# Attention and a SwiGLU block in one kernel: output-weight sums of 768 columns at other places, one load moved between two others, three small moves and a third store queue at the end

## The chip, the core and the metric

The kernel runs on one core of one Trainium2 chip. The metric is the device time of one execution in microseconds (us). A core has five engines, each with its own program and its own order: TensorE (PE; its weight loads, PEld, run beside its matmuls), VectorE (DVE), ScalarE (ACT), GpSimd (POOL) and SyncE (SP). SP, ACT and POOL can ask for DMA transfers. TensorE's results lie in PSUM, whose banks are handed round among the tiles of a pool: a tile can be written when the last reader of its bank's former tile is done.

## The reference

```
scores = q @ k.T / sqrt(64)              # 8 batches, 12 heads, 448 tokens, 64 columns a head
attn   = softmax(scores)
x      = (attn @ v), heads side by side  # 3584 tokens x 768
g      = x @ w_gate                      # 768 x 1536
out    = (g * sigmoid(g) * (x @ w_val)) @ w_out   # 1536 x 768
```

Inputs and output are float32. The kernel computes in float16 with float32 accumulation; transfers issued by POOL convert on the way.

## The kernel before

**Attention.** Two heads make a pair; there are 48 pairs, six to a batch. `load_qk16` and `load_v` let POOL fetch q, k and v. For pairs 0 to 10, `prep` turns q and k with TensorE (L249, L272); from pair 11 on POOL copies them into one tile (L231, L208) and SP issues DMA transposes (L234 to L240; L210 and L214). `qk` multiplies keys by queries a chunk of keys at a time (L329; from pair 12 on L299, and L311 for the chunk that two pairs share) and ACT takes the exponential of each (L337, L319). `pv` multiplies by the values with a column of ones (L355, L363, L390), takes the reciprocal of the sums (L374, L415) and scales (L376, L416). The result is turned into X, 768 x tokens: with TensorE and a copy (`turn_x`, L446 and L453) for pairs below 12, by SP's transposes (L455, L459) behind. In the first two batches the last 64 columns of each pair are turned together by `turn_rests` (L472, L479).

**The SwiGLU block.** Tokens go in eight blocks of 384 or 512. A `Step` is one block with 128 of the 1536 hidden columns: six matmuls for the gate, six for the value (L513), a tanh on ACT (L537), the product `t` = (tanh + 1) x gate (L553), and the product `hts` of `t` and the value (L561), both on DVE. `run_fv` runs one step; `run_pair` runs two whose gates stand ahead of both values.

**The output.** Block 0 and single chunks are multiplied plainly (`plain_out`, L581 and L588). All else goes by groups (`out_group`): 2 x 2 blocks of tokens and hidden halves are multiplied with seven products in the place of eight (L610), from sums of hidden values (`h_sums`, L498 to L501) and sums of output weights (`out_sums`, L487 to L490), which are made once. The parts are put together by ACT (L650, L629) and DVE (L651, L653, L657, L663). The next six matmuls of TensorE behind L657 overwrite what L657 reads.

**Where the sums are made.** The order on every engine is written out by hand. Sums stand in the lists `wsums` and `sums`; `add_sum` takes the next from `sums` and puts it at that place in DVE's order. `run_o`, which runs one output step of block 0, moves four of `wsums` and makes them when less than two output steps are left; the others are made inside the steps of block 1 in the same manner as the sums of hidden values later. One weight sum takes the 384 columns of one of six pairs of hidden blocks.

**The order of the loads.** POOL issues DMAs in program order, and its transfers land in that order here. `wq` names the pair at whose entry the weights are asked for: `("o", 0)` at pair 6, `("o", 1)` at pair 7, 1152 KB each. On the entry of pair 8 the kernel asks for q and k of pair 14 (`load_qk16(pr + LA, 1)`, LA = 6). In the program as built, POOL's DMAs take eight semaphores in turn, so that a DMA waits for the landing of the one eight places before it.

**The end.** The last group runs two halves of the columns side by side. Each of its four parts, named by z (which 128 tokens) and qw (which half), is stored when it is ready, as two DMAs: z = 0, qw = 1 by ACT, the three others by SP.

Of the kernel before, what the change touches and what calls it, by code (L numbers as in the profile page):

```python
# [39 lines left out]
def kernel(  # L40
# [10 lines left out]
    nc = tc.nc  # L51
    B, H, S, D = q.shape
# [11 lines left out]
    OH = DM // 2  # L64
# [48 lines left out]
    NH = NFB // 2  # L113
# [3 lines left out]
    Tsum = [x.rearrange("p (c m) -> p c m", c=NH) for x in spare]  # L117
# [4 lines left out]
    QW = OH // 2  # L122

    wo_all = consts.tile([128, 2, NFB, OH], FP16, name="wo")
# [3 lines left out]
    qkT = {}  # L128
# [90 lines left out]
    def prep(pr):  # L219
        if pr >= QUAD:  # L220
            return prep_quad(pr)
        rq, rk = raw[pr]
        if pr == 0 or pr >= NPE:
            qk16 = attp.tile([128, 2, NC, 2, D], FP16, tag="qk16", name="qk16", bufs=3)[0:P]
            for t, src in enumerate((rq, rk)):
                dst = qk16[:, 1 - t].rearrange("p c h d -> p h c d")
                if pr == 0:
                    nc.vector.tensor_copy(dst[:, 0], src[:, 0])
                    nc.scalar.activation(dst[:, 1], src[:, 1], AF.Copy)
                else:  # L230
# [12 lines left out]

        def turn0():
            for t in range(2):
                tp = ps_s.tile([128, 2, 512], FP32, tag="s", name="tp")
                for c in range(NC):
                    for hx in range(2):
                        nc.tensor.matmul(  # L249
                            tp[ts(hx, 64), c // 2, ds(c % 2 * P, P)],  # L250
                            lhsT=qk16[:, 1 - t, c, hx],
                            rhs=ident[0:P, 0:P],
                            start=True,
                            stop=True,
                        )
                dst = qkT[pr][:, ts(1 - t, S)].rearrange("p (a x) -> p a x", a=2)
                nc.vector.tensor_copy(dst[:, 0], tp[:, 0, 0 : 2 * P])
                nc.scalar.activation(dst[:, 1], tp[:, 1, 0 : 2 * P], AF.Copy)
                if t == 0:
                    tq = tp  # L260
            nc.vector.tensor_copy(qkT[pr][:, 2 * S :], tq[:, 0, 0:D])

        def turn():
            if pr < FIRST + 2:
                tp = ps_s.tile([128, 2, 1024], FP16, tag="s", name="tp")[:, 0]
            else:
                tp = ps_f.tile([128, 1024], FP16, tag="f", name="tp")
            for i in range(2 * NC + 1):
                t, c = (1 - i // NC, i % NC) if i < 2 * NC else (0, 0)
                for hx in range(2):  # L270
                    src = raw[pr][t][:, hx, c, :]
                    nc.tensor.transpose(tp[ts(hx, 64), ts(i, P)], src, ident[0:P, 0:P])  # L272
            nc.vector.tensor_copy(qkT[pr][:], tp[:, 0 : 2 * S + D])

        return turn if pr else turn0
# [205 lines left out]
    gate_small = [False]  # L481

    def out_sums(c):
        b11, b12, b21, b22 = (wo_all[:, :, f, ts(i, QW)] for f in (c, NH + c) for i in range(2))
        t1, t2, t3, t4 = (t[:, c].rearrange("p (h m) -> p h m", h=2) for t in Tsum)
        return [
            lambda: nc.vector.tensor_sub(t1, b12, b11),  # L487
            lambda: nc.vector.tensor_sub(t2, b22, t1),
            lambda: nc.vector.tensor_sub(t3, b22, b12),
            lambda: nc.vector.tensor_sub(t4, b21, t2),  # L490
        ]
# [70 lines left out]
                self.hts[:, self.fb, 0:n], self.t1[:, 0:n], 0.5 * HS, self.vp[:, 0:n], ALU.mult, ALU.mult  # L562
            )

    def store(osb, kk, l0, n, m0, w, queue=nc.sync):
        l = l0
        while l < l0 + n:
            b, j = divmod(l, S)
            turned = D if b + NB * kk < QUAD // NHP else 0
            c, p0 = divmod((j + turned) % S, P)  # L570
            m = min(P - p0, l0 + n - l, (MQ if turned and j < MQ else S) - j)
            dst = out[ts(NB * kk + b, S), :].rearrange("(p c) m -> c p m", c=NC)[c, p0 : p0 + m]
            src = osb[l - l0 : l - l0 + m]
            queue.dma_start(dst[:, ds(m0, w)], src[:, ds(m0, w)])
            l += m

    def plain_out(kk, c0, hts, ch, m0, w, osb):
        op = ps_f.tile([128, 512], FP32, tag="f", name="op")
# [24 lines left out]
    def out_group(kk, c0, hts, t, qw, osb, last=False, own=False):  # L603
        x, y, w = ts(2 * t, 128), ts(2 * t + 1, 128), ts(qw, QW)
        g = ps_s.tile([128, 2, 512], FP32, tag="s", name="og")
        a, c, b = g[:, 0, 0:QW], g[:, 0, QW:OH], g[:, 1, 0:QW]
# [24 lines left out]
        def stored(z):  # L631
            l0 = c0 + (2 * t + z) * 128
            if last:
                store(osb[z], kk, l0, 128, qw * OH, OH, nc.sync if z or not qw else nc.scalar)
            elif qw:
                store(osb[z], kk, l0, 128, 0, DM)

# [19 lines left out]
        part = nc.vector.scalar_tensor_tensor(d, b, 1.0 / HS, p15[:], ALU.mult, ALU.add)  # L657
# [20 lines left out]
    with tc.manual_schedule():  # L678
# [6 lines left out]
        for vo in Vts:  # L685
# [19 lines left out]
            3: [("qk", 9, 1), ("qk", 10), ("g", 2), ("v", 2)],  # L705
            4: [("g", 3), ("v", 3), ("qk", 12)],
            6: [("V", 3), ("o", 0)],
            7: [("o", 1)],
        }

        def emit(item):
# [12 lines left out]

        groups = []
        sums = []
        wsums = [f for c in range(NH) for f in out_sums(c)]
        steps = []

        def pair_groups(kk, c0, hts, t, last=False):  # L730
# [38 lines left out]
        def add_sum(n=1):  # L769
            for _ in range(n):  # L770
                if sums:
                    sums.pop(0)()

        def run_fv(quiet=False, more=0):
            step = fvq.pop(0)
            step.gate()
            add_sum(more)
            step.value(0)
            if not quiet:
                add_sum()  # L780
            step.finish()
            if not quiet:
                add_sum()
            return 2 * step.time

        def run_pair(small=0):
            one, two = fvq.pop(0), fvq.pop(0)
            one.gate()
            two.gate()
            one.value(0)  # L790
            one.gated()
            two.gated()
            one.finish()
            add_sum(small)
            two.value(0)
            add_sum()
            two.finish()
            return 4 * one.time

# [8 lines left out]
        def run_o():  # L808
            gen, t = oq.pop(0)
            next(gen)  # L810
            if len(oq) < 2 and not groups and wsums:
                sums.extend(wsums[:4])
                wsums[:4] = []
                add_sum(4)
            return t

        def run_group(nf, inside=None, gate_first=False):
            gen = groups.pop(0)[0](gate_first)
            for _ in range(nf - 1):
                run_fv()  # L820
            step = fvq.pop(0)
            if gate_first:
                step.gate()
                add_sum()
            next(gen)
            if not gate_first:
                step.gate()
                add_sum()
            if inside:
                inside()  # L830
                next(gen)
            step.value(0)
            add_sum()
            step.finish()
            add_sum()
            if not inside:
                next(gen)

        def run_budget(budget):
            while (fvq or oq) and budget > 0:  # L840
                if not fvq:
                    budget -= run_o()
                elif len(fvq) > 1 and fvq[0].at[1] and 2 * fvq[0].time < budget <= 4 * fvq[0].time:
                    budget -= run_pair(1)
                else:
                    budget -= run_fv(more=1)
            return budget

        def left():
# [12 lines left out]
        for u in range(FIRST * NC):  # L862
            pr, c = divmod(u, NC)
# [22 lines left out]
        queue = []  # L886
# [12 lines left out]
        while g < last or queue:  # L899
            n = 2 if g < WIDE * NC else 3  # L900
# [16 lines left out]
        def open_products(rests):  # L917
            for p0 in rests:
                pv_open(p0)
                pv_rest(p0)  # L920
            return []
# [6 lines left out]
        for x, (chunks, todo) in enumerate(plan):  # L928
# [14 lines left out]
            for n, (pr, c) in enumerate(ordered):  # L943
                if n == 2 and after_group:
                    rests = open_products(rests)
                qk(pr, c)
            open_products(rests)
            end = min([y for y in adds if y > x] + [len(plan) + 1])
            if x == 0:
                turn_x(4)  # L950
# [40 lines left out]
            else:  # L991
# [10 lines left out]
                    run_steps(nf)  # L1002
                for _ in range(no):
                    run_o()
            if x == 1:
                turn_rests(0)
            while turns:
                turn_x(turns.pop(0))
            if XPE - 1 in [p0 for _, p0 in todo]:
# [54 lines left out]
```

## Time and profile before

| What | us |
|---|---|
| median of 3 runs (lowest, highest) | 445.86 (442.65, 447.48) |
| the profiled execution, its own time | 446.76 |
| its span from first to last instruction | 445.0 |
| TensorE busy, share of the span | 430.9 (97%) |
| VectorE, ScalarE, GpSimd busy | 263.3, 222.9, 180.2 |
| granted TensorE clock, mean | 0.994 |
| sums of output weights, L487 to L490, 24 of 384 columns | 13.2 busy |

Durations and places below come from the one profiled execution, in microseconds from the start of its span. The time of an execution is 1.8 us longer than the span. TensorE's "busy" holds matmuls one after the other; a gap in it is shown in brackets with what ended it. The "granted clock" is the share of its full clock that TensorE had in a stretch.

### The profile page before, as it was taken

The numbers are of one execution on the slowest core, as the hardware profiler recorded it, in microseconds if no ns is written. First come the engines' busy times: TensorE is split into PE (matmuls) and PEld (weight loads), VectorE is DVE, ScalarE is ACT, GpSimd is POOL, SyncE is SP. The second block draws the span as 40 slices with busy tenths as digits, with TensorE's granted clock in tenths as the row PEclk, the third lists the DMA queues.
The fourth block names the chain that finished last, engine by engine and source line by source line (L and its number), as shares of the span: only waits on it lengthen the run. The fifth ranks groups of instructions, "written<-read, shape, count | busy, mean of one in ns | idle before, by whom it ended". The sixth has DMA issues, their size and how long they took to land.

```text
span 445.0 us, 11025 instructions
## 1 busy us (share of the span) xinstructions
PE 430.9 (97%) x4456; PEld 274.9 (62%) x4456; DVE 263.3 (59%) x611; ACT 222.9 (50%) x332; POOL 180.2 (40%) x299
## 2 busy tenths in 40 slices
PE   8999999898999999999999999999999999999995
PEld 3665565544446686674756776774756778565494
DVE  4666562586777755655556755564556665654562
ACT  6975667455456546454545554546464642222221
POOL 8755714997874645535533362823000000000000
PEclk9999999899999999999999999999999999999999
DMA  9999999999999789984899669954142012202014
GB/s 138 189 199 201 199 173 144 149 199 184 134 140 96 89 135 125 160 106 67 109 132 125 89 99 139 160 107 66 34 109 53 12 42 62 73 1 72 0 41 140
DMA packets 108500, 49.98 MB, mean 112 GB/s; under 512 B 60832, under 2 KB 105120, under 8 KB 108448
## 3 DMA queue, kind: packets, MB, share of 16 engines
q0 software_dynamic: 46832, 24.56, 49.6%
q1 hardware_dynamic: 61456, 24.52, 30.6%
q8 instruction: 35, 0.57, 0.5%
q10 hardware_dynamic: 160, 0.20, 0.2%
q14 instruction: 17, 0.14, 0.1%
HBM read 49.55 MB, written 11.01 MB: 136 GB/s over the span
## 4 chain that ended last, share of the span: by engine, by line
PE 74%; DMA 13%; DVE 4%; POOL 4%; issue 2%; ACT 1%; SPq 0%; DVEq 0%; POOLq 0%
PE gp L513 21%; PE vp L513 20%; PE og L610 16%; PE acc L390 8%; DMA qkraw<-in_k_dram 5%; PE s L299 5%; DMA wv<-in_moe_w_val_dram 4%; PE op L581 4%; DMA wg<-in_moe_w_gate_dram 2%; POOL qkraw L171 2%; PE s L311 1%; DMA qkT<-qk 1%; ACT E L319 1%; DVE hts L561 1%; POOL vraw L182 1%
## 5 line engine op out<-in xcount | busy, mean ns | idle before, releaser
L513 PE MATMUL gp<-X,wg 128*128 128x384 f16 (+1 forms) x576 | 123.3, 353 | 0.0
L513 PE MATMUL vp<-X,wv 128*128 128x384 f16 (+1 forms) x576 | 123.2, 352 | 0.0
L319 ACT ACTIVATE E<-s 128x896 f16<-128x896 f32 x126 | 106.7, 917 | 32.5 <-PE s L299 20.5
L537 ACT ACTIVATE sg<-gp 128x384 f32<-128x384 f32 (+1 forms) x96 | 52.4, 546 | 92.2 <-PE gp L513 86.3
L553 DVE SCALAR_TENSOR_TENSOR t<-sg,gp 128x384 f32<-128x384 f32 (+1 forms) x96 | 59.5, 620 | 64.7 <-ACT sg L537 64.3
L513 PEld LDWEIGHTS <-wv 128*128 128x128 f16 x576 | 56.3, 98 | 51.9
L513 PEld LDWEIGHTS <-wg 128*128 128x128 f16 x576 | 53.6, 98 | 45.7 <-issue 2.6
L208 POOL COPY qk<-qkraw 128x512 f16<-128x512 f16 x72 | 43.6, 655 | 92.6 <-DMA qkT<-qk 91.5
L561 DVE SCALAR_TENSOR_TENSOR hts<-t,vp 128x384 f16<-128x384 f32 (+1 forms) x96 | 59.5, 620 | 8.9 <-PE vp L513 0.8
L148 POOL DMA_DIRECT2D vraw<-in_v_dram x72 | 44.6, 651 | 16.1 <-DVE xt L376 7.3
L390 PEld LDWEIGHTS <-E 128*128 128x128 f16 (+1 forms) x1152 | 37.8, 97 | 14.6 <-issue 8.7
L390 PE MATMUL acc<-vo,E 128*128 128x65 f16 (+1 forms) x1152 | 43.3, 193 | 3.0 <-DVE hts L561 3.0
L610 PEld LDWEIGHTS <-hts 128*128 128x128 f16 x528 | 44.0, 98 | 2.1 <-issue 1.1
L337 ACT ACTIVATE E<-s 112x896 f16<-112x896 f32 x48 | 40.7, 917 | 7.9 <-PE s L329 7.7
L148 POOL DMA_DIRECT2D qkraw<-in_k_dram x70 | 43.1, 641 | 2.3 <-DMA wg<-in_moe_w_gate_dram 1.2
L415 DVE RECIPROCAL R<-acc 128x4 f32<-128x4 f32 x72 | 12.7, 177 | 37.7 <-PE acc L390 37.6
L629 ACT ACTIVATE osb<-og 128x384 f32<-128x384 f32 x22 | 10.8, 491 | 45.3 <-PE og L610 38.8
L171 POOL DMA_DIRECT2D qkraw<-in_q_dram x44 | 30.6, 696 | 4.7 <-DMA vraw<-in_v_dram 1.2
L416 DVE TENSOR_TENSOR xt<-acc,R 128x256 f16<-128x256 f32 x72 | 30.5, 424 | 2.5
L299 PE MATMUL s<-qkT 64*128 64x448 f16 x216 | 30.0, 353 | 1.7 <-DMA qkT<-qk 1.7
L610 PE MATMUL og<-wo,hts 128*128 128x192 f16 x264 | 29.0, 246 | 0.0
L610 PEld LDWEIGHTS <-hsum 128*128 128x128 f16 x300 | 25.7, 98 | 2.3
(78 smaller groups left out, 391.5 us busy)
## 6 DMA issues: line engine op xcount, KB each, us to landing
vraw<-in_v_dram POOLq DMA_DIRECT2D x72, 64.0 KB, 4.7
qkraw<-in_q_dram POOLq DMA_DIRECT2D x41, 112.0 KB, 4.2
qkraw<-in_k_dram POOLq DMA_DIRECT2D x68, 64.0 KB, 4.4
wg<-in_moe_w_gate_dram POOLq DMA_DIRECT2D x8, 288.0 KB, 10.1
wv<-in_moe_w_val_dram POOLq DMA_DIRECT2D x8, 288.0 KB, 10.2
wo<-in_moe_w_out_dram POOLq DMA_DIRECT2D x2, 1152.0 KB, 20.2
out_dram<-osb SPq DMA_DIRECT2D x7, 288.0 KB, 4.2
out_dram<-osb SPq DMA_DIRECT2D x6, 336.0 KB, 3.4
```

The costliest lines, as they stand in the source:

```text
L148: eng.dma_start(dst[ts(s, 64)], rows)
L171: nc.gpsimd.dma_start(dst, flat.rearrange("h (p c) d -> p h (c d)", c=NC))
L208: nc.gpsimd.tensor_copy(dst.rearrange("p c h d -> p h c d"), src)
L299: nc.tensor.matmul(s[:, hx, 0:S], lhsT=t[ts(hx, 64), ts(c + low(pr, hx), 128)], rhs=t[ts(hx, 64), ds(NC * 128, S)], start=True, stop=True,)
L319: nc.scalar.activation(e[:, 0 : 2 * S].rearrange("p (h q) -> p h q", h=2), s[:, :, 0:S], AF.Exp, scale=sm_scale)
L337: nc.scalar.activation(e[:, :, 0:S], s[0:P, :, 0:S], AF.Exp, scale=sm_scale)
L390: nc.tensor.matmul(acc[:, ts(j, D + 1)], lhsT=e[rows, ds(hx * S + j * 128, 128)], rhs=Vts[pr % NV][rows, hx, col, 0 : D + 1], start=first, ...
L513: nc.tensor.matmul(dst[:, 0:n], lhsT=wslice(kind, self.fb, cb), rhs=X[kk][:, cb, ds(c0, n)], start=(cb == 0), stop=(cb == NCB - 1),)
L537: nc.scalar.activation(self.sg[:, 0:n], gp[:, 0:n], AF.Tanh, scale=0.5)
L553: nc.vector.scalar_tensor_tensor(self.t1[:, 0:n], self.sg[:, 0:n], 1.0, self.gp[:, 0:n], ALU.add, ALU.mult)
L561: nc.vector.scalar_tensor_tensor(self.hts[:, self.fb, 0:n], self.t1[:, 0:n], 0.5 * HS, self.vp[:, 0:n], ALU.mult, ALU.mult)
L610: nc.tensor.matmul(dst, lhsT=lhs(n), rhs=rhs(n), start=first and n == 0, stop=n == NH - 1, skip_group_check=True)
```

## The change

Seven places are edited.

1. `out_sums` takes two hidden blocks at once, so that a sum has 768 columns and there are 12; their order is now the first two kinds for all columns, then the last two. `run_o` moves three at a time.
2. In `run_pair` with `small`, one sum stands between the two `t` products, and none between the two `hts`; `run_fv` has no extra sum behind the gate.
3. In `run_group` the last sum is made behind the end of the group (`next(gen)`).
4. The second output weight is asked for at pair 8, behind q and k of pair 14.
5. `turn_rests(0)` stands behind the scores of step 2, and no longer at the end of step 1.
6. In `turn0` the copy of the first 64 columns stands directly behind the first of the two copies.
7. In the last group's stores the larger of the two DMAs goes first, and the part z = 1, qw = 0 is issued by POOL.

```diff
-                if t == 0:
-                    tq = tp
-            nc.vector.tensor_copy(qkT[pr][:, 2 * S :], tq[:, 0, 0:D])
+                if t == 0:
+                    nc.vector.tensor_copy(qkT[pr][:, 2 * S :], tp[:, 0, 0:D])
...
     def out_sums(c):
-        b11, b12, b21, b22 = (wo_all[:, :, f, ts(i, QW)] for f in (c, NH + c) for i in range(2))
-        t1, t2, t3, t4 = (t[:, c].rearrange("p (h m) -> p h m", h=2) for t in Tsum)
+        b11, b12, b21, b22 = (
+            wo_all[:, :, ds(f, 2), ts(i, QW)].rearrange("p h c m -> p c h m") for f in (c, NH + c) for i in range(2)
+        )
+        t1, t2, t3, t4 = (t[:, ds(c, 2)].rearrange("p c (h m) -> p c h m", h=2) for t in Tsum)
...
+        if large_first:
+            parts.sort(key=lambda part: -part[0])
+        for _, dst, src in parts:
+            queue.dma_start(dst, src)
...
-                store(osb[z], kk, l0, 128, qw * OH, OH, nc.sync if z or not qw else nc.scalar)
+                store(osb[z], kk, l0, 128, qw * OH, OH, (nc.sync, nc.scalar, nc.gpsimd, nc.sync)[2 * z + qw], True)
...
-            7: [("o", 1)],
+            8: [("o", 1)],
...
-        wsums = [f for c in range(NH) for f in out_sums(c)]
+        wsums = [f for part in (slice(0, 2), slice(2, 4)) for c in range(0, NH, 2) for f in out_sums(c)[part]]
...
-        def run_fv(quiet=False, more=0):
+        def run_fv(quiet=False):
             step = fvq.pop(0)
             step.gate()
-            add_sum(more)
             step.value(0)
...
             one.gated()
+            if small:
+                add_sum()
             two.gated()
             one.finish()
-            add_sum(small)
             two.value(0)
-            add_sum()
+            if not small:
+                add_sum()
             two.finish()
...
             if len(oq) < 2 and not groups and wsums:
-                sums.extend(wsums[:4])
-                wsums[:4] = []
-                add_sum(4)
+                sums.extend(wsums[:3])
+                wsums[:3] = []
+                add_sum(3)
...
             step.finish()
-            add_sum()
             if not inside:
                 next(gen)
+            add_sum()
...
-                    budget -= run_fv(more=1)
+                    budget -= run_fv()
...
             open_products(rests)
+            if x == 2:
+                turn_rests(0)
...
-            if x == 1:
-                turn_rests(0)
```

More of the change, by code (lines that the diff above doesn't have):

```diff
@@ L563, in finish, with store @@
             )
-    def store(osb, kk, l0, n, m0, w, queue=nc.sync):
+    def store(osb, kk, l0, n, m0, w, queue=nc.sync, large_first=False):
+        parts = []
         l = l0
@@ L572, in store @@
             dst = out[ts(NB * kk + b, S), :].rearrange("(p c) m -> c p m", c=NC)[c, p0 : p0 + m]
-            src = osb[l - l0 : l - l0 + m]
-            queue.dma_start(dst[:, ds(m0, w)], src[:, ds(m0, w)])
+            parts.append((m, dst[:, ds(m0, w)], osb[l - l0 : l - l0 + m, ds(m0, w)]))
             l += m
+        if large_first:
+            parts.sort(key=lambda part: -part[0])
+        for _, dst, src in parts:
+            queue.dma_start(dst, src)
     def plain_out(kk, c0, hts, ch, m0, w, osb):
```

## The prediction

> **What bounds the kernel now.** I read the page's busy table first, then TensorE's waits, then the timelines around each wait. TensorE (PE) is the bound nearly everywhere, so the change can win only what PE loses: gaps, and matmuls at a lower clock.
>
> ```profile
> PE 430.9 (97%) x4456; PEld 274.9 (62%) x4456; DVE 263.3 (59%) x611; ACT 222.9 (50%) x332; POOL 180.2 (40%) x299
> ```
>
> PE's own waits, from the table of waits (engine, line, releaser: us in total, times, longest):
>
> ```profile
> PE acc L390 <- DVE hts L561: 3.0, 4, 1.1
> PE s L299 <- DMA qkT<-qk: 1.7, 1, 1.7
> ...
> PE og L610 <- DVE osb L657: 0.4, 1, 0.4
> ```
>
> The second is the dearest. PE's timeline (start, us, line, in brackets the gap before) and the stretches around it (PE busy, PEld busy, DVE, ACT, POOL, then granted clock, DMA):
>
> ```profile
> 78.19 0.55 PE L299 MATMUL s<-qkT 64*128 64x448 f16 x4
> 80.45 0.36 PE L299 MATMUL s<-qkT 64*128 64x448 f16 x2 [1.71 <-DMA qkT<-qk]
> 80.64 1.59 PE L390 MATMUL acc<-vo,E 64*128 64x65 f16 x32
> 82.31 5.13 PE L581 MATMUL op<-wo,hts 128*128 128x384 f16 x24
> 87.37 0.38 PE L311 MATMUL s<-qkT 64*64 64x448 f16 x4
> ...
> 82.30:84.50 2.20, 2.19 (x7) 1.04 (x8) 2.13 (x8) 0.00 (x0) 2.20 (x5) 0.50 2.27 182
> ```
>
> The score chunk at 80.45 is the first of pair 14. PE stood still 1.71 us, and then the granted clock fell to 0.50 until 84.5: the 24 output matmuls took 5.13 us, against 4.07 for the same 24 at 66.99. Why pair 14 was late stands in POOL's timeline:
>
> ```profile
> 47.99 1.02 POOL L202 DMA_DIRECT2D wo<-in_moe_w_out_dram  x1
> 50.11 0.67 POOL L171 DMA_DIRECT2D qkraw<-in_q_dram  x1
> ...
> 71.99 0.59 POOL L148 DMA_DIRECT2D vraw<-in_v_dram  x1 [7.24 <-DMA qkraw<-in_k_dram]
> 73.10 1.17 POOL L208 COPY qk<-qkraw 128x512 f16<-128x512 f16 x2 [0.52 <-issue]
> ```
>
> Both output weights (1152 KB each, landing after 16.7 and 23.7 us, so at 63.7 and 71.7) are ahead of pair 14's q and k, which land at 72.2 to 72.9. POOL idles till then, its copies for pair 14 start at 73.10, SP's transposes at 73.74 and 75.02, and the second lands 5.3 us later, at 80.3.
>
> The other large wait is VectorE's (DVE): two weight sums stand between the two products `hts`, and POOL's copies lengthen the first.
>
> ```profile
> 93.12 0.69 DVE L561 SCALAR_TENSOR_TENSOR hts<-t,vp 128x512 f16<-128x512 f32 x1
> 93.56 1.33 POOL L208 COPY qk<-qkraw 128x512 f16<-128x512 f16 x2
> 93.72 1.39 DVE L487 TENSOR_TENSOR E<-wo 128x384 f16<-128x384 f16 x1
> 94.89 0.19 PE L390 MATMUL acc<-vo,E 64*128 64x65 f16 x1
> 95.15 0.36 DVE L488 TENSOR_TENSOR E<-wo,E 128x384 f16<-128x384 f16 x1
> 95.42 0.68 DVE L561 SCALAR_TENSOR_TENSOR hts<-t,vp 128x512 f16<-128x512 f32 x1
> ```
>
> PE's next accumulator takes the bank that the second `hts` frees, so PE waits 1.08 us until 96.16; likewise 1.12 at 104.28, 0.58 at 115.35, 0.20 at 127.02.
>
> **The change, part by part**, against the profiled execution (446.76 us, span 445.0).
>
> *A. Pair 14 between the output weights.* POOL's second 1.02 us issue moves behind two copies and three DMAs. In queue order pair 14 now lands just behind the first weight: 63.7 plus the 1.2 us that its three transfers needed behind the second one, 64.9. The DMAs of POOL take eight semaphores in turn, so each waits for the one eight places before. The second V load of pair 12 thus no longer waits for the second output weight but for pair 14's q, and goes at 64.75 behind the first (64.16). Copies at 65.4 instead of 73.10; transposes issued at about 66.1 and 67.3. They then run beside the second weight, where the last pair's second transpose took 12.3 us: 79.6 at worst; at 5.3 us it would be 72.6. I take 77: pair 13's last transpose landed at 72.0 under the same load, and two more follow. PE wants it at 78.74, so the gap goes. Gain: 1.71; the products at 80.64 to the output matmuls at 82.31 shrink from 1.67 to 1.47 (at full clock the first reciprocal comes 0.78 after the start and normalising ends 0.64 later, plus 0.05 of release); the output matmuls 5.13 - 4.07 = 1.06. Sum **2.97**. Bounds: 0 (the transposes gain nothing) to 3.0.
>
> A rule against this sum: the Trainium skill, "TensorE: Matmul & The Clock Gate", Part 1, lets the clock drop after an idle window of about 3.4 us, so a 1.71 us gap need not cost clock at all. By the rule alone A would be worth 1.71 us. The row shows 0.50 behind this gap and 1.00 behind gaps of 1.1, and the row decides.
>
> What is late next: POOL's next-but-few DMA (pair 16's second k load) now inherits the second weight's semaphore and waits for it. The second weight lands 1.2 us later, at 72.9 (first needed by PE at 75.66, a step that is unchanged, so hidden). Pair 15's copies follow three issues and one more landing later at about 75.0, against 77.19: 2.1 us earlier. Its second transpose landed at 79.17 + 6.8 = 86.0; it lands at about 83.9 now. PE asks for it at 87.37 - 2.97 = 84.4. That margin of 0.5 us is the thinnest in the change.
>
> *B. Weight sums.* 24 sums of 384 columns become 12 of 768. The 384-wide ones took 0.34 to 0.36 us undisturbed; the 768-wide sums of the hidden values take 0.553. If the strided operands are no slower than there (bounds: 0.55, and 0.95 at twice the narrow slope, 0.35 + 3 x 0.2), DVE saves 24 x 0.35 - 12 x 0.55 = 1.8 us, off PE's path. What counts is the place: three pairs now have their sum between the two `t` products, and both `hts` stand together. In the pair above: sum 91.84 to 92.4, `t` when its tanh is there (92.45 to 93.14), `hts` to 93.8, then the second from 94.3 to 95.0; PE asks at 95.08. If POOL's copies hold the sum for 1.57 us (the longest 384-wide row), the second `hts` ends at 95.5, and PE loses 0.45. So B is worth 2.78 less 3 x 0 to 3 x 0.45: 1.4 to 2.8. I take **2.2**, nearer to the undisturbed row, since POOL's copies fill 1.3 of each 4.1 us. The six sums behind the output steps (3.4 us on DVE, against 4.0) keep their cover, the output matmuls, until the reciprocal at 88.87; without it each would cost its 0.55.
>
> *C. Sums behind groups.* In three even blocks the in-place sum (0.55 us) stands ahead of the output's L657, and PE's next six-matmul group starts late. Groups follow each other by 0.49 there, but 147.08 to 147.87, 249.03 to 250.06 and 351.22 to 352.01 are 0.79, 1.03 and 0.79: 0.30 + 0.54 + 0.30, **1.1**; I take 1.0. Behind L663 the sum has a free stretch until the next reciprocal. Bounds 0 to 1.1.
>
> *D. Last stores.* SP issues the stores of part z = 1, qw = 0 at 439.65 only because the issue before them ran 1.70 us; they go to POOL at about 438.0. SP's last large store then starts at about 440.0 instead of 441.0. SP's rows land 1.9 to 3.3 us after issue, POOL's loads 2.8 us in a quiet stretch (300 to 340) and 4.7 as the page's median. Last landing now 443.6; then 443.1 (SP), 442.9 (ACT), and 438.0 + 2 x 0.65 + 2.8 to 4.7 = 442.1 to 444.0 (POOL). Gain **0.5**, bounds -0.4 to 0.7. The skill's "DMA: Bandwidth & Descriptors", SWDGE vs HWDGE vs iDMA, calls POOL's path the slower to set up (a microsecond against 0.6 to the first byte); by that POOL's store would land 0.4 later, still not last.
>
> *E. Start.* The rests of block 0 go behind two score chunks: PE's 0.19 wait (L472 for `t`) is covered by 0.37 us of scores, and the accumulator's bank is free at 37.19, before it is asked for. L261 moves into DVE's 0.28 us pause ahead of the second L257, and the first score starts 0.13 earlier. **0.3**, bounds -0.2 to 0.4.
>
> Sum: 2.97 + 2.2 + 1.0 + 0.5 + 0.3 = 7.0. 446.76 - 7.0 = **439.8 us**. The median shown, 445.86, is 0.9 lower and would give 438.9; the profile's gaps may be its own, so I keep 439.8. Within about 1% (4.46 us) a measurement can't tell this kernel from no change.
>
> **The rivals.**
> 1. *Pair 14 or 15 is late all the same.* The transposes lose to the second weight, or pair 15 eats the margin: a wait of 1 to 2 us at 78.74 or 84.4, with or without the low clock. A shrinks to 0 to 1.5: 441.3 to 442.8. For: transposes issued at 54.7 to 59.7 needed 12 us beside the weights. Against: 11 us are there.
> 2. *The sums do not do what they say*: the strided 768-wide form runs at 0.95 us or meets POOL's copies each time. B falls to 1.4 or below, with pair 14 repaired: 440.6 to 442.
> 3. *Slower.* POOL stands at pair 16's k load until the second output weight has landed, with pair 13's V, pair 15's copies and all later loads behind it. Pair 15's transposes land 10.9 us after the weight. If pair 14's transposes hold the weight up beyond 73.5, PE waits at 84.4 by the difference, and behind a gap like 80.45's loses 1.3 more at half clock. From a landing at 79.2 on (5.7 of wait and 1.3) all 7.0 are gone; at 81 it is 448.6. For: weight and transposes now share the DMA engines. Against: it landed 8.0 us behind the first, with three pairs' transposes beside it.
>
> **How the numbers follow.** Forecast (437.5 to 441.3) 0.58; rival 1 0.18; rival 2 0.14, a third of it under 441.4; rival 3 0.10. Faster by over 1% means below 441.4: 0.58 + 0.05 = 0.63, less 0.03 for scatter in the runs (442.65 to 447.48 before); slower by over 1% is rival 3 beyond 450.3 with scatter, 0.06; the rest, 0.34, is within. The range goes from 437.0 (all upper ends, 8.0 us, off the profile 438.8, off the median 437.9, less scatter) to 444.0 (rival 1's end and scatter).
>
> **What would show it.** A: no wait for qkT on PE, copies of pair 14 near 65, granted clock 1.00 from 80 to 85, and POOL's new wait until about 73. B: 12 sums near 0.55 us, PE's wait for `hts` down to about 0.5 in all. C: group distance 0.49 at all three. D: last store 443.6 - 440.0 or less behind the last L663. I am wrong if the qkT wait only moves to pair 15, or if POOL's copies meet the new sums.

## The result, and the profile after

| | before | after |
|---|---|---|
| median of 6 runs, us | 445.32 (442.23 to 447.48) | 440.01 (439.08 to 440.95) |
| the profiled execution, its own time | 446.76 | 440.09 |
| its span | 445.0 | 438.3 |
| mean granted clock | 0.994 | 0.998 |

The ratio of the two is 0.9889, with a 95% interval of 0.9845 to 0.9934: about 5 us less, between 2.9 and 6.9. The predicted time was 439.8.

The new table of TensorE's waits (engine, line, releaser: us in total, times, longest):

```profile
PE wp L134 <- DVE warm L685: 1.0, 1, 1.0
...
PE op L586 <- DVE xt L415: 0.4, 1, 0.4
PE s L298 <- DVE X L478: 0.3, 1, 0.3
PE s L328 <- DVE qkT L257: 0.3, 1, 0.3
PE acc L389 <- DVE hts L562: 0.2, 1, 0.2
```

The wait for pair 14's transposes is gone, that for `osb` is gone, and that for `hts` is 0.2 in place of 3.0 us. TensorE's timeline around pair 14, and the stretch that had the clock of 0.50 (columns as before):

```profile
79.02 0.55 PE L298 MATMUL s<-qkT 64*128 64x448 f16 x4
79.89 0.37 PE L298 MATMUL s<-qkT 64*128 64x448 f16 x2 [0.32 <-DVE X L478]
80.08 1.14 PE L389 MATMUL acc<-vo,E 64*128 64x65 f16 x32
81.58 4.07 PE L586 MATMUL op<-wo,hts 128*128 128x384 f16 x24 [0.37 <-DVE xt L415]
85.58 0.38 PE L310 MATMUL s<-qkT 64*64 64x448 f16 x4
```

```profile
82.30:84.50 2.20, 2.20 (x15) 1.31 (x14) 2.17 (x4) 0.49 (x1) 2.20 (x5) 1.00 1.25 162
```

From the chunk ahead of pair 14's to the shared chunk (L311, now L310) it is 6.56 us in place of 9.18. A small gap of 0.32 is left, and its releaser is new. VectorE's timeline says why:

```profile
77.71 0.77 DVE L189 COPY vo<-vraw 128x512 f16<-128x512 f16 x1 [0.15 <-DMA vraw<-in_v_dram]
78.81 0.56 DVE L452 CAST X<-xtp 128x384 f16<-128x384 f32 x1 [0.34 <-PE xtp L445]
79.29 0.55 DVE L478 CAST X<-rtp 128x384 f16<-128x384 f32 x1
```

The score chunk needs the bank that L478 reads. L478 stands behind L452, and both stand behind the copy of pair 12's V (L189). That load now lands behind the second output weight, at 77.62 (before: 74.91). In this profile it is not what L452 waits for last: VectorE is done with L189 at 78.48 and waits 0.34 us more for TensorE's own transposes (L445). On POOL the new wait is where it was expected, but it ends later:

```profile
67.27 1.17 POOL L208 COPY qk<-qkraw 128x512 f16<-128x512 f16 x2 [0.42 <-issue]
...
75.16 0.59 POOL L148 DMA_DIRECT2D qkraw<-in_k_dram  x1 [5.52 <-DMA wo<-in_moe_w_out_dram]
76.52 1.18 POOL L148 DMA_DIRECT2D vraw<-in_v_dram  x2 [0.77 <-DMA qkraw<-in_q_dram]
77.69 1.26 POOL L208 COPY qk<-qkraw 128x512 f16<-128x512 f16 x2
```

The second weight landed at 74.88, and pair 15's copies start at 77.69, no earlier than before (77.19). Their second transpose landed at 85.42, and TensorE asked for it at 85.58.

One pair of steps of block 1 on VectorE:

```profile
89.97 0.55 DVE L490 TENSOR_TENSOR E<-wo 128x768 f16<-128x768 f16 x1
90.67 0.69 DVE L554 SCALAR_TENSOR_TENSOR t<-sg,gp 128x512 f32<-128x512 f32 x1
91.33 0.69 DVE L562 SCALAR_TENSOR_TENSOR hts<-t,vp 128x512 f16<-128x512 f32 x1
92.63 0.69 DVE L562 SCALAR_TENSOR_TENSOR hts<-t,vp 128x512 f16<-128x512 f32 x1 [0.61 <-PE vp L514]
```

The sum takes 0.55 us with 768 columns, and in front of the second `hts` VectorE now waits 0.61 us for TensorE, where TensorE waited for it.

By stretches the 6.67 us between the two spans are: start of the span to the chunk ahead of pair 14's, **0.83 lost** (78.19 to 79.02); from there to the shared chunk, 2.62 gained; from the next gate matmul (L513, now L514; 89.03 and 87.25) to the end of block 1 (135.04 and 130.70), 2.56 gained; the three places of edit 3 together, 1.1 gained; from TensorE's last matmul to the end of the span, 1.1 gained (5.5 to 4.4); 0.1 lies between.

### The profile page after: what moved, and what is told of

Same layout as the page of the kernel before. It is cut to its first block, busy times and chain, and to the rows that moved or that the text cites. A ratio compares the mean times of both kernels' runs of the same rounds, so it can differ in the third digit from the quotient of the medians.

```text
span 438.3 us, 11013 instructions
## 1 busy us (share of the span) xinstructions
PE 430.0 (98%) x4456; PEld 274.3 (63%) x4456; DVE 256.9 (59%) x599; ACT 222.8 (51%) x332; POOL 182.1 (42%) x301
## 4 chain that ended last, share of the span: by engine, by line
PE 94%; DVE 4%; ACT 1%; issue 0%; DVEq 0%
PE gp L514 25%; PE vp L514 24%; PE og L615 17%; PE acc L389 8%; PE op L586 5%; PE s L298 5%; PE acc L354 2%; PE s L328 2%; PE tp L271 1%; PE s L310 1%; PE wp L134 1%; DVE hts L562 1%; DVE t L554 1%; PE acc L362 1%; ACT sg L538 1%; DVE qkT L272 0%
## 5 line engine op out<-in xcount | busy, mean ns | idle before, releaser
L514 PE MATMUL gp<-X,wg 128*128 128x384 f16 (+1 forms) x576 | 123.3, 353 | 0.0
L514 PE MATMUL vp<-X,wv 128*128 128x384 f16 (+1 forms) x576 | 123.2, 352 | 0.0
L514 PEld LDWEIGHTS <-wv 128*128 128x128 f16 x576 | 56.3, 98 | 51.9
L514 PEld LDWEIGHTS <-wg 128*128 128x128 f16 x576 | 53.6, 98 | 45.7 <-issue 2.6
L580 POOL DMA_DIRECT2D out_dram<-osb x2 | 1.1, 550 | 132.1 <-DVE osb L668 132.1
```

What stands on the lines that cost most here:

```text
L514: nc.tensor.matmul(dst[:, 0:n], lhsT=wslice(kind, self.fb, cb), rhs=X[kk][:, cb, ds(c0, n)], start=(cb == 0), stop=(cb == NCB - 1),)
```

## The experiments

All are edits of the changed kernel or of the one before. Two distances of one timeline serve as a ruler for A and for B. The **A stretch** runs from the first matmul of block 0's third output step to block 1's first gate matmul; the **B stretch** runs from there to the first matmul of the first output group.

| kernel | median us (runs) | ratio to before, 95% | A stretch | B stretch | waits for hts |
|---|---|---|---|---|---|
| before | 445.32 (6) | | 17.20 | 53.62 | 3.0 |
| before, again | 447.45 (1) | | 18.62 | 53.40 | 2.7 |
| before + edit 4 | 443.18 (12) | 0.9963 [0.9939, 0.9986] | 16.25 | 52.24 | 1.0 |
| before + edits 1, 2 | 443.51 (12) | 1.0007 [0.9980, 1.0033] | 15.66 | 51.21 | 0.2 |
| after - edit 4 | 441.27 (8) | 0.9925 [0.9898, 0.9952] | 18.41 | 51.06 | 0.2 |
| after - edits 1, 2 | 440.15 (6) | 0.9887 [0.9852, 0.9921] | 15.40 | 51.45 | 0.7 |
| after, wide sums at the old place | 439.80 (6) | 0.9888 [0.9857, 0.9919] | 15.08 | 51.12 | 0.2 |
| after, narrow sums at the new place | 440.17 (6) | 0.9896 [0.9868, 0.9925] | 14.78 | 51.06 | 0.2 |
| after | 440.01 (6) | 0.9889 [0.9845, 0.9934] | 14.58 | 51.06 | 0.2 |
| after, again | 439.60 (6) | 0.9872 [0.9835, 0.9909] | 14.70 | 51.07 | 0.2 |

Each ratio is to runs of the kernel before on the same chip. The kernel before itself ran 58 times beside these: median 444.2, from 441.96 to 448.05. Both its profiles (446.76 and 447.45) come from the upper quarter. Three more runs stand below: one execution each with small edits taken back (441.69) and with a copy moved (440.27), and one with gaps put in (576.64), whose time is not compared.

**Edit 4 alone taken back.**

```diff
-            8: [("o", 1)],
+            7: [("o", 1)],
```

> The changed kernel with edit 4 alone taken back: the second output weight is asked for at pair 7 again. Theory (A is worth 2.6 us, a gap and the clock behind it): TensorE waits about 1.7 us for the first score chunk of pair 14, the granted clock then falls to about 0.5 for some 2 us and the 24 output matmuls behind it take about 5.1 us in place of 4.07; 440.0 + 2.6 = 442.6 us. Rival 1 (the clock window of the Trainium skill: a gap this short costs no clock): the gap comes back, the clock stays at 1.00, the 24 matmuls take 4.1 us, 441.5 us. Rival 2 (the wait was that one execution's own): no gap, 440.0 us.

TensorE's timeline:

```profile
80.64 0.36 PE L298 MATMUL s<-qkT 64*128 64x448 f16 x2 [2.47 <-DMA qkT<-qk]
80.83 1.14 PE L389 MATMUL acc<-vo,E 64*128 64x65 f16 x32
82.34 5.75 PE L586 MATMUL op<-wo,hts 128*128 128x384 f16 x24 [0.37 <-DVE xt L415]
```

Both terms of the theory are there: a gap, now 2.47 us, and a low clock (0.70 on average over the 5.68 us of the output matmuls, which take 1.68 longer). Still the median rose by only 1.3 us over the changed kernel's. Among the eight runs the profiled one is the second longest: 442.88 and 443.06, and then six from 440.35 to 441.47.

**Edit 4 alone made.**

```diff
-            7: [("o", 1)],
+            8: [("o", 1)],
```

> The kernel before with edit 4 alone. Theory: A stands by itself, so no wait for pair 14 and no low clock near 80 us, and 445.3 - 2.6 = 442.7 us. TensorE reaches this stage some 0.8 us earlier than in the changed kernel while the transfers do not, and pair 15 had only 0.16 us to spare there, so a wait of 0 to 0.8 us at the first chunk of pair 15 is expected by this theory too. Rival (the gap only moves on): TensorE waits 1.5 us or more for pair 15, with the low clock behind it, and the time stays at 444.5 to 445.3 us.

The ratio is 0.9963, some 1.6 us. The clock is 1.00 throughout the stretch. TensorE reached it early here and met both next limits: 0.94 us for L479 (behind pair 12's V) and 0.68 us for pair 15 at 85.86. So A's gain, as this profile shows it, is what lies between pair 14's landing and the next two transfers, and what TensorE gains ahead of them is lost at them. The waits for `hts` came down to 1.0 without any edit of the sums.

**The sums: width and place.** First the wide sum at the old place:

```diff
-            if small:
-                add_sum()
             two.gated()
             one.finish()
             two.value(0)
-            if not small:
-                add_sum()
+            add_sum()
```

> The changed kernel with its sums of 768 columns at the old place: in each pair of steps the one sum stands between the two products hts, not between the two products t. Theory of the place (the prediction's): POOL's copies meet the sum there and stretch it to 1.4 to 1.6 us, as they did the first of two narrow ones, so that TensorE waits 0.8 us for hts in two or more of the four pairs; 441.5 to 442.5 us. Rival, the number: one sum of 0.55 us fits into the 0.61 us for which VectorE waits for the second value anyway, no matter where it stands; waits for hts of 0.4 us or less in all, 440.0 to 440.3 us.

Then two narrow sums behind each other at each new place:

```diff
+        return [(lambda f=f, g=g: (f(), g())) for f, g in zip(narrow(c), narrow(c + 1))]
```

> The changed kernel with sums of 384 columns again, two behind each other at each of the new places. Theory of the place: two take 0.70 us in place of 0.55, the second t starts at most 0.1 us later than it could, and the 0.61 us before the second hts hides even a stretched sum, so TensorE's waits for hts stay at 0.4 us or less in all; 440.0 to 440.4 us. Rival, the width: two narrow sums are lengthened by POOL's copies to 1.7 us or more, as at 93.72 and 101.80 of the kernel before, and the waits of about 1 us come back at two places; 442 us.

Then edits 1 and 2 taken back together (here their core), and, the other way round, made alone:

```diff
-            wo_all[:, :, ds(f, 2), ts(i, QW)].rearrange("p h c m -> p c h m") for f in (c, NH + c) for i in range(2)
+        b11, b12, b21, b22 = (wo_all[:, :, f, ts(i, QW)] for f in (c, NH + c) for i in range(2))
...
             one.finish()
+            add_sum(small)
             two.value(0)
-            if not small:
-                add_sum()
+            add_sum()
```

> The changed kernel with edits 1 and 2 taken back: 24 sums of 384 columns, two between the two products hts. Theory of the prediction: the waits for hts come back to about 3 us in all, 442.2 to 442.8 us. Rival, the meeting: what two narrow sums cost depends on whether POOL's copies fall on them, which changes with the place of the transfers; waits for hts of about 1 us in all as in the run with edit 4 alone, 440.8 to 441.2 us.

> The kernel before with edits 1 and 2 alone: the sums of 768 columns at their new places. Theory of the prediction (A and B are separate gains): the waits for hts fall from 2.7 to 3.0 us to 0.2 to 0.5, and the time is 2 us or more below the kernel before, 442.3 to 442.8 us. Rival, the meeting (what the narrow sums cost comes from pair 14's lateness, which pushes POOL's copies onto them, and it went away with edit 4 alone): here the lateness is still there, so B gains its 2 to 2.8 us in this kernel too, although it gained 1 us at most beside edit 4; A and B then share a gain and their single gains add up to more than the two together. If the wait for pair 14 stays at 1.7 to 2.9 us and the time still falls by 1 us or less, something behind 135 us gives it back.

The first two have B stretches of 51.12 and 51.06 and the changed kernel's time: neither the width nor the place is needed by itself. But in neither run did POOL's copies stretch a sum inside a pair beyond 0.83 us, so the expected meeting did not take place, and what a sum of 1.4 us and more would cost at the one place or the other is not shown. What costs in the profiles is two narrow sums between the two `hts` when POOL's copies fall on them. VectorE in the kernel before, again:

```profile
94.61 0.35 DVE L487 TENSOR_TENSOR E<-wo 128x384 f16<-128x384 f16 x1
95.00 1.40 DVE L488 TENSOR_TENSOR E<-wo,E 128x384 f16<-128x384 f16 x1
96.32 0.68 DVE L561 SCALAR_TENSOR_TENSOR hts<-t,vp 128x512 f16<-128x512 f32 x1
```

POOL copied from 94.85 to 96.18 there. The same two sums, at the same place of the order, in the changed kernel without edits 1 and 2, where POOL had copied from 90.04 to 91.28:

```profile
91.78 0.35 DVE L486 TENSOR_TENSOR E<-wo 128x384 f16<-128x384 f16 x1
92.17 0.36 DVE L487 TENSOR_TENSOR E<-wo,E 128x384 f16<-128x384 f16 x1
92.47 0.69 DVE L560 SCALAR_TENSOR_TENSOR hts<-t,vp 128x512 f16<-128x512 f32 x1
```

Undisturbed the two fit into the pause that VectorE has anyway. Where pair 14 is on time the copies mostly miss them, and B has little left to gain: 0.4 us of the B stretch (51.45 against 51.06), nothing in the time. Where pair 14 is late, the two profiles show 2.2 and 2.4 us (53.40 and 53.62 against 51.21), but the time of edits 1 and 2 alone is that of the kernel before, 1.0007. So their gain is 0.9 us at most by that interval. Why the 2.2 to 2.4 us of the profiles are not in the times is not settled; one likely reason is that both profiles of the kernel before are long executions, while the one of edits 1 and 2 alone (441.81) is the shortest of its twelve; there may be more.

**Gaps put in.** Behind the gate of every second step VectorE writes a scratch tile, and one extra product waits for it:

```diff
+        for _ in range(size):
+            nc.vector.memset(warm[:], 0.0)
+        nc.tensor.matmul(step.vp[:, 0:64], lhsT=warm[:], rhs=warm[:, 0:64], start=True, stop=True)
```

> The changed kernel with 19 gaps made on purpose: behind the gate of every second step from the 60th on VectorE writes a small scratch tile 5 to 45 times, and one extra product of TensorE waits for it (nothing is left out; the total time is not compared). Theory of the prediction (length alone): behind every gap of 1.7 us or more the granted clock falls to 0.50 for about 2 us, behind those of 1.1 us or less it stays at 1.00. Rule of the Trainium skill (TensorE: Matmul & The Clock Gate, Part 1): no fall behind gaps under about 3.4 us. Third theory, the phase: the gate looks at stretches of fixed length whose edges have nothing to do with the gap, so gaps of one length sometimes cost clock and sometimes not, and the longer ones more often; then the 1.06 us of part A were chance.

The nineteen gaps came out at 1.96 to 9.62 us. The extra product of four of them in TensorE's timeline:

```profile
371.39 0.20 PE L516 MATMUL vp<-warm 128*128 128x64 f16 x1 [1.97 <-DVE warm L515]
...
383.73 0.20 PE L516 MATMUL vp<-warm 128*128 128x64 f16 x1 [2.72 <-DVE warm L515]
...
514.78 0.20 PE L516 MATMUL vp<-warm 128*128 128x64 f16 x1 [2.73 <-DVE warm L515]
...
527.31 0.20 PE L516 MATMUL vp<-warm 128*128 128x64 f16 x1 [3.50 <-DVE warm L515]
```

and the 8 us behind each, where the granted clock is the third number from the end:

```profile
371.39:379.39 8.00, 8.00 (x69) 4.75 (x70) 2.79 (x8) 3.46 (x5) 0.00 (x0) 0.79 0.03 6
383.73:391.73 8.00, 7.17 (x77) 4.45 (x77) 4.76 (x12) 3.74 (x6) 0.00 (x0) 1.00 0.25 66
...
514.78:522.78 8.00, 8.00 (x45) 4.99 (x46) 2.62 (x6) 1.09 (x2) 0.00 (x0) 0.79 0.24 72
527.31:535.31 8.00, 5.38 (x25) 2.29 (x25) 3.73 (x14) 1.19 (x2) 0.00 (x0) 1.00 0.00 0
```

The clock fell behind both gaps of about 1.96 us, behind one of two of 2.7, behind neither of 3.38 and 3.50, and behind all thirteen of 4.15 and more. A clock of 0.79 over 8 us is a loss of 1.7 us of full clock, or 3.4 us at half. Length alone does not decide it: the prediction's reading of its row falls, and the third theory stands.

The clock record of the trace shows what does. The seventeen falls of this run (the last at its end) begin 13.65, 17.07, 20.48, 23.89 or 34.13 us behind each other, which is 4, 5, 6, 7 and 10 times 3.413 us. Cut the run along this grid: at full clock, the clock fell at the end of every stretch of 3.41 us in which TensorE had stood idle for 1.96 us or more, and at the end of none with 1.94 or less. The gap of 1.97 us lies whole in one stretch (368.74 to 372.15); the one of 3.50 is parted by an edge at 525.75 into 1.94 and 1.56. By an estimate from these numbers a gap of 3.9 us can't be parted any more so that both parts stay short, and the shortest of the thirteen is 4.15. In the kernels themselves the limit is less sharp: 1.71 us in one stretch was enough in the kernel before, 1.73 was not in the tuned kernel below, whose gap of 2.93 us is parted into 1.21 and 1.73, nor 1.97 behind the last matmul of the changed kernel's second profile.

The Trainium skill, "TensorE: Matmul & The Clock Gate", Part 1, has the clock fall after an idle window of about 3.4 us; these gaps contradict that as the least gap (1.96 was enough). It also says that this window runs free of the kernel, and the grid agrees.

**The kernel before, again.** 

> The kernel before, unchanged, for a second profile. Theory, the places and their prices belong to the kernel: the wait for pair 14 is 1.7 to 2.5 us, the 24 output matmuls behind it take more than 5 us, and TensorE's waits for hts are 3.0 us in all. Rival, they belong to that one execution: the wait for pair 14 is there, but the clock may stay at 1.00 behind it, and the waits for hts are about 1.0 us as in the run with edit 4 alone.

The wait for pair 14 was 2.93 us, the 24 output matmuls took 5.50, and the waits for `hts` were 2.7: as the theory said. In the run of edits 1 and 2 alone pair 14 was 1.40 us late and the 24 matmuls took 4.08. So the clock fell behind three of the four waits for pair 14 (1.71, 2.47, 2.93, not 1.40); in the fourth, only 1.14 us of TensorE's idle time lie in the stretch of the grid. The 58 executions agree: 26 under 444 us had a mean granted clock of 0.9973, 13 above 446 had 0.9939. The changed kernel's twelve had 0.9988, and a spread of 1.9 us where the kernel before has 6.

**Edits 3, 6 and the third queue taken back** (one execution, 441.69 us).

```diff
-                    nc.vector.tensor_copy(qkT[pr][:, 2 * S :], tp[:, 0, 0:D])
+                    tq = tp
+            nc.vector.tensor_copy(qkT[pr][:, 2 * S :], tq[:, 0, 0:D])
...
+            add_sum()
             if not inside:
                 next(gen)
-            add_sum()
...
-                store(osb[z], kk, l0, 128, qw * OH, OH, (nc.sync, nc.scalar, nc.gpsimd, nc.sync)[2 * z + qw], True)
+                store(osb[z], kk, l0, 128, qw * OH, OH, nc.sync if z or not qw else nc.scalar, True)
```

> The changed kernel with three small edits taken back, read at three places that are far apart: edit 3 (the last sum again ahead of the end of the group), edit 6 (the copy of the first 64 columns again behind both others) and the POOL queue of edit 7 (three of the four last parts on SP again, the larger DMA still first). Theory for 3: the distances of the groups at three places go from 0.50 back to 0.8 to 1.05 us, 0.9 to 1.1 us in all. For 6: from the end of the last transposition of q and k to the first score 0.61 us as in the kernel before, against 0.74 to 0.84 with the edit; so the edit lost 0.1 to 0.2 us and gained none. Rival for 6: 0.75 and more in this kernel too. For 7, theory of the queue: the last landing lies 3.5 us or more behind VectorE's last instruction, as before; rival, the order of the two DMAs does it: 2.7 to 3.0 us, as in the changed kernel.

Edit 3: each of the three places has 0.30 us more again, 0.9 in all. Edit 6: the first score starts 0.61 us behind the last transposition, as before; with the edit it is 0.74 to 0.95 in eight profiles. The edit loses 0.1 to 0.3 us. Edit 7: the last landing is 3.05 us behind VectorE's last instruction (before 3.69, after 2.73), and the end of the span 4.62 (before 5.04, after 3.92). So the order of the two DMAs is worth about 0.4 us and the third queue about 0.7. That is one execution: the end of the span lies 4.77 to 5.04 behind VectorE's last instruction in the four profiles without edit 7, and 3.46 to 4.27 in the nine with all of it.

**Beyond the change.** Two kernels go after pair 12's V and pair 15. The first only moves L189 behind the two copies into X:

```diff
-            for p0 in vcopies.get(x, []):
-                if p0 not in early:
+            late_v = [p0 for p0 in vcopies.get(x, []) if p0 not in early]
+            rests1 = XPE - 1 in [p0 for _, p0 in todo]
+            if not rests1:
+                for p0 in late_v:
                     copy_v(p0)
...
-            if XPE - 1 in [p0 for _, p0 in todo]:
+            if rests1:
                 turn_rests(1)
+                for p0 in late_v:
+                    copy_v(p0)
```

> The changed kernel with one move in VectorE's order: the copy of pair 12's V (L189) stands behind the two copies into X that follow it, so that these no longer wait for the V load. Theory (what is late next is pair 12's V, landing behind the second output weight at about 77.5 us, and VectorE stands before it): TensorE's wait for the copy of the rests, 0.3 to 0.9 us in the runs so far, is 0.1 us or less; the first chunk of pair 14 starts at about 78.3 us if the start is an early one, and pair 15, which lands when it did, is then waited for by 0.3 to 0.7 us. Rival (the wait is for the matmuls of the rests themselves, not for the load): 0.8 us as before.

The second also loads pair 13's V ahead of pair 16's q and k, these behind pair 15's copies, and takes edit 6 back:

```diff
+                if pr == 11:
+                    load_qk16(pr + LA - 1, 1)
-                if 14 <= pr + LA < NPAIR:
+                if 14 <= pr + LA < NPAIR and pr != 10:
```

> A version meant to beat both: the changed kernel, with pair 12's V copied as in the run before, pair 13's V loaded ahead of pair 16's q and k and these behind pair 15's copies on POOL (so that pair 15's copies stand behind no wait for the second output weight), and edit 6 taken back. Theory: pair 15's copies start at about 76.6 us in place of 77.2 to 77.7, its second transpose lands before it is asked for, no wait of more than 0.3 us is left between 77 and 90 us, and the first score stands 0.61 us behind the last transposition; 0.5 to 1.0 us less than the changed kernel, about 439.3 us. Rival (the transfers bind, not the order): pair 15 lands no earlier than 84.4 us, TensorE waits for it by what it has gained, and the time is that of the changed kernel within 0.3 us.

> The changed kernel again, on the same chip as the version meant to beat it. Theory: 440.0 us; a slow start like that of its first profile (half clock until 10.2 us) is chance, so this profile has the first gate matmul between 28.3 and 28.8 us in place of 29.72, and TensorE waits longer, 0.6 to 0.9 us, for the copy of the rests, so that little of the 1.2 us is seen at the end. Rival (edits 5 and 6 make the start slow): 29.7 us again.

The move alone left 0.32 us, which the matmuls of the rests and the two copies need by themselves (the same 0.32 as in both profiles of the changed kernel), and a wait of 0.62 came up at 131.76 for pair 17's transposed X; 440.27. The tuned one did what it should up to 90 us: pair 15 landed at 83.65 and was asked for at 83.99, the shortest A stretch for so early a start (14.60). Then:

```profile
129.11 0.98 PE L515 MATMUL gp<-X,wg 128*128 128x384 f16 x5
133.02 0.32 PE L515 MATMUL gp<-X,wg 128*128 128x384 f16 x1 [2.93 <-DMA X<-xt]
```

Pair 16's copies had moved from 81 to 84.06 us on POOL, SP's transposes stand behind them in its order, and pair 17's X was asked for at 128.90 in place of 124.94. Median 440.50 against 439.60 for the changed kernel on the same chip: no better. Beyond 80 us the changed kernel is held by the chain of POOL's copies and SP's transposes with little to spare, and what TensorE gains ahead of it is lost at the next of its transfers. The changed kernel again shows the other side. Its start is 0.96 us earlier than in its first profile (first gate matmul at 28.76 against 29.72), and its span 1.0 shorter.

The difference of the two starts is the clock again. TensorE in the first profile of the changed kernel:

```profile
5.21 0.61 PE L134 MATMUL wp<-warm 128*128 128x512 f16 x1
6.12 0.94 PE L328 MATMUL s<-qkT 64*128 64x448 f16 x4 [0.30 <-DVE qkT L257]
...
8.52 0.61 PE L134 MATMUL wp<-warm 128*128 128x512 f16 x1
...
9.90 0.60 PE L134 MATMUL wp<-warm 128*128 128x512 f16 x2
10.44 0.36 PE L328 MATMUL s<-qkT 64*128 64x448 f16 x2
```

and in the second:

```profile
5.21 0.39 PE L134 MATMUL wp<-warm 128*128 128x512 f16 x1
6.17 0.75 PE L328 MATMUL s<-qkT 64*128 64x448 f16 x4 [0.57 <-DVE qkT L257]
```

The same matmul of 512 columns takes 0.61 us in one, up to 8.52 us into the span, and 0.39 in the other; at 9.90 two of them, one begun before the other is done, take 0.60 together. The column of the granted clock says 1.00 for both. The run with the gaps put in started slowly too, until about 10.3 us. Carried back from the falls of each trace, the grid of 3.413 us has edges at 9.82 and 10.33 us in these two and at 4.99 in the second profile, and there the matmuls turn fast. So the length of the slow start goes by the grid as well. Both slow starts are among the eight profiles with edits 5 and 6, and none is among the six others; that these edits make them likelier is not shown, nor ruled out.

## Why the prediction was right, point by point

The time was right, and against the profiled execution so was the sum: 6.67 us where 7.0 were forecast. Its base was not, nor were several of its steps.

**The base.** The terms were read from one execution of 446.76 us. Of 58 later ones the median is 444.2, so that execution was 2.5 us longer than usual, and some of what made it so (the fallen clock, the copies on the sums) is just what parts A and B were paid for. Against the usual execution the change is worth 4 to 5 us (444.2 less 440.0, or 444.8 less 439.6 on one chip). The prediction kept 439.8 and said that the gaps might be the profile's own; its result was saved by setting those gaps against the time that had them. In part that is luck: by the times the parts are worth less than 7.0, and the base was too long by nearly as much. The agreement of the profiles is partly luck too, since the five parts were off by -0.35, +0.36, +0.1, +0.6 and -1.1.

- **A, 2.97 forecast.** 2.62 in the two profiles, about 1.6 in the times (0.9963 alone; 0.9889 against 0.9925 beside the rest). The transposes landed at 77.41 where 77 was taken, by two errors that cancel: the second was issued at 69.20 in place of 67.3 and took 8.2 us in place of 9.7. The step that failed is "so the gap goes": 0.32 to 0.94 us of it stay. 0.32 of that is what the transposes of the rests and the two copies into X need by themselves, which pair 14's lateness had hidden. The rest, in the runs where TensorE comes early, is pair 12's V, whose issue was followed and whose landing was not: it comes 2.7 us later, and the copies stand behind it. The clock term of 1.06 was sized rightly for one execution (1.68 and 1.43 in two others); whether it is paid depends on where the gap lies in the grid of 3.41 us.
- **What is late next.** The second weight landed at 74.88, not 72.9: the first was itself 1.1 us later (64.78), and the second came 10.1 us behind it in place of 8.1 plus 1.2, of which pair 14's transfers took 2.3. So pair 15's copies were not 2.1 us earlier but 0.5 later, and the margin of 0.5 us was 0.16. It held in that profile; with an earlier start it was short by 0.6 to 0.7 in two runs. Rival 1 was so much the nearest.
- **B, 2.2 forecast.** 2.56 in the profiles, 0 to 0.9 in the times. The step that failed is "What counts is the place": beside A the wide sum costs nothing at the old place either, and two narrow ones cost nothing at the new. The row of 1.39 us was a meeting with POOL's copies, and in the profiles with edit 4 these mostly miss the sums. B was priced as if the meeting stayed when A was made, and A and B were added.
- **C, 1.0 forecast.** 1.1 in the profiles and 0.9 when taken back.
- **D, 0.5 forecast.** 1.1. The POOL store landed 2.43 and 2.65 us after issue, below the 2.8 taken as the least. SP's last store went 0.39 us behind VectorE's last instruction in place of 1.06. That putting the larger DMA first gains about 0.4 by itself was not priced.
- **E, 0.3 forecast.** A loss of 0.8 in the profile; the slow clock at the start, which the second profile of the same kernel has not, is about 1.0 of it. Without that, nothing is left to see: the chunk ahead of pair 14's starts at 77.62 to 78.19 in the four profiles with neither edit 5 nor 6, and at 77.62 to 78.06 in the six with both and a fast start. The wait of L471 (0.19) went as forecast. "The first score starts 0.13 earlier" failed: L260 waits 0.42 us for ScalarE's copy (L258) and so delays the second L257, which the score needs.

Rival 3 did not come near: the weight landed at 74.88, and all would have been lost from 79.2 on. By the times A is about 1.6 us and B 0 to 0.9, so of 5 us some 2.5 to 3.4 are left for C, D and E, of which the timelines show 2.2; the intervals, 1 to 2 us to each side, are too wide to say more.

## What to carry to other kernels

Set the gaps of a profile against the time of that same execution, but ask of each gap whether it belongs to the kernel or to the execution: a low clock and a meeting of two engines may be there in one execution and not in the next. A second profile need not tell it. Here it showed the same gaps, since it was a long execution too; the times of many executions and the edits taken one by one told it. When a load is moved ahead of another, follow every load behind it to its landing and to the engine that stands waiting for it, not only to its issue. Where a chain of transfers sets the pace, what the compute engine gains is lost at the next transfer of that chain, and small edits ahead of it show nothing in the time.

## What the runs showed of the hardware that was not expected

- The clock of TensorE may fall behind a gap of 1.96 us and not fall behind one of 3.50; it fell behind all thirteen of 4.15 us and more. The falls begin on a grid of 3.413 us that does not start with the kernel, and what decides is the idle time inside one stretch of it: 1.96 us was enough and 1.94 was not in the run with nineteen gaps. Behind the short gaps a fall cost 1.7 us of full clock.
- At the start, matmuls ran at half speed until 9.8 and 10.3 us in two profiles and until some 4 to 6 us in the twelve others, while the column of the granted clock said 1.00.
- Two sums of 384 columns take 0.35 us each or, under POOL's copies, up to 1.73; the one of 768 took 0.55 undisturbed and 1.74 under them (102.16 in the run of edits 1 and 2 alone). Width is no protection.
- A POOL store of 112 and 16 rows landed 2.4 and 2.7 us after issue, SP's and ScalarE's beside it 2.3 to 2.5: at the end of the kernel POOL's queue was as good as theirs.
